# Retention's state products cut into two halves of 64 tokens, on four quadrants of the array

## The chip, the cores and the metric

The kernel runs on one NeuronCore of a Trainium2 chip. Its engines run beside each other and wait for one another by semaphores: TensorE (PE, with its weight loads as PEld), VectorE (DVE), ScalarE (ACT), GpSimd (POOL) and SyncE (SP, which issues the DMAs). The metric is the device time of one execution in microseconds (us), lower is better.

## The reference, cut to what matters

Three layers follow one another: a retention over 768 tokens in 2 batches and 8 heads of 64, then a softplus layer (512 to 2048 to 512), then a SwiGLU layer. The change touches only the retention:

```python
for t in range(S):                                    # S = 768
    state = gamma * state + einsum('bhd,bhe->bhde', k[:, :, t], v[:, :, t])
    y[:, :, t] = scale * einsum('bhd,bhde->bhe', q[:, :, t], state)
```

## The kernel before

The 768 tokens of a batch are cut into 6 chunks (CPB) of 128, so that there are 12 chunks g = 0 to 11 in the program; c is the chunk's number in its batch. A chunk goes through these steps, each of which is a function:

- `turn` (L536) transposes q and k on TensorE; `turned` (ScalarE, L543) and L538 (VectorE) copy them out of PSUM as `at`.
- `scores` (L555) multiplies them into two banks `sc`; its `masked` (VectorE, L559, two instructions of 128x512) writes the masked scores to SBUF, also called `at`.
- `update` (L565 to L583) forms the chunk's addition to the state. It has 8 products, one for each head: the stationary operand is k, 128 tokens by 64, the moving one v, 128 tokens by 64. Two heads share a column of the 128x256 result `u`, one on partitions 0 to 63 and one on 64 to 127. Then `added` writes the new state: a copy where c is 0 (L580), else `u` plus the faded old state (L582). The last chunk of a batch has no update, so that there are 10.
- `fade` (GpSimd, L592) multiplies the new state by the decay, for the next `added`.
- `outputs` (L607) forms y in two banks: first the old state times q, 64x64 weights with 128 moving columns on the four quadrants of the array (`y<-at,state`), where c is over 0; then the masked scores times v (`y<-at,v`, 128x64 weights). The first product of the first kind writes bank 0 of the two, the second bank 1.

In the trace each product of these has two rows on TensorE, so an update has 16.

Chunks 0 to 3 are written out singly (L697 to L751). In the first two the update follows the y products and the scores follow it; in chunk 2 it stands between the scores and the y products; in chunk 3 between the y products and the first product of the next layer (`h`, L645). Chunks 4 to 11 go in pairs through `batch` (L753): transposes of both chunks, scores of both, updates of both, then the outputs of both. In `batch` VectorE's order behind the first update is written out: `added` of the first chunk, one instruction for the weights of a later layer (L433, in two of the four batches), `masked` of the second chunk, and so on. Between the batches stand products `h` of the first layer. From 71.5 us on a planner orders the rest (L960).

PSUM has 8 banks. `bank` hands out the one that was taken longest ago:

```python
oldest = list(range(8))                 # L289
def bank(name, to=oldest):
    i = oldest.pop(0)
    to.append(i)
```

So each further bank that is taken moves all the later ones along, and what a product must wait for is whoever read that bank last.

Of the kernel before, what the change touches and what calls it, by code (L numbers as in the profile page):

```python
# [12 lines left out]
ALU = mybir.AluOpType  # L13
# [240 lines left out]
def retention_softplus_swiglu(ctx: ExitStack, tc: tile.TileContext, q, k, v, w_in, w_out,  # L254
                              w_gate, w_val, w_out2, rms_g, decay, out):
    nc = tc.nc
    B, H, S, D = q.shape
# [8 lines left out]
    NP = H // 2  # L266
# [24 lines left out]
# [3 lines that stand above are left out]
        return ps.tile([P, N], F32, tag=f"ps{i}", name=name)  # L294
# [26 lines left out]
    faded = fd[:, 2 * CPB * H + P:2 * CPB * H + P + NP * D].rearrange("p (j d) -> p j d", j=NP)  # L321
# [243 lines left out]
    def update(g):  # L565
        c = g % CPB
        kk, vv = qkv[g][1], qkv[g][2]
        if c == CPB - 1:
            return lambda: None
        u = bank("u")[:, 0:NP * D].rearrange("p (j t) -> p j t", j=NP)  # L570
        for j in range(NP):
            for e in range(2):
                h = 2 * j + e
                nc.tensor.matmul(u[e * D:(e + 1) * D, j, :], lhsT=kk[:, h, :], rhs=vv[:, NP * e + j, :],  # L574
                                 start=True, stop=True, skip_group_check=True)

        def added():
            new = state[(c + 1) % 2]
            if c == 0:
                nc.vector.tensor_copy(new, u)  # L580
            else:
                nc.vector.tensor_tensor(out=new, in0=u, in1=faded, op=ALU.add)  # L582
        return added  # L583

    def step_u(g):
        update(g)()
        qkv.pop(g)
# [141 lines left out]
    for do in (low32, size, shift, bits):  # L729
        do()  # L730
    masked = scores(3)
    added = update(2)
    added()
    total()
# [10 lines left out]
    nc.sync.dma_start(out=rg, in_=rms_g.rearrange("(k p) -> p k", p=P))  # L745
    parted = outputs([3])
    added = update(3)
    parted()
    added()
# [497 lines left out]
    def lone_gated(nm, f):  # L1247
        h = psum(f"h_{nm}")
        project(h, weight_of(nm, f), XN)
        key = LONE, f  # L1250
        if nm == "w_gate":
            t = pr[key] = r2("t")
            if LONE not in root:
                moved("A", t, h)
                waiting.append(lambda: (less(t, t, root[LONE], ALU.mult), silu(t)))
                return
            else:
                add("V", V_2, lambda e: nc.vector.tensor_tensor(out=t.tile, in0=h.tile, in1=root[LONE].tile, op=ALU.mult),
                    reads=[h, root[LONE]], writes=[t], opens=[t])
            silu(t)  # L1260
        else:
            t = pr[key]
            add("V", V_2, lambda e: nc.vector.tensor_tensor(out=t.tile, in0=h.tile, in1=t.tile, op=ALU.mult),
                reads=[h, t], writes=[t])
            split(key, t)
# [124 lines left out]
    for p in range(NPR):  # L1390
        g, v = Gated("w_gate", p), Gated("w_val", p)
        h = [lambda f=f, nm=nm: lone_gated(nm, f) for nm in ("w_gate", "w_val") for f in (2 * p, 2 * p + 1)]
# [17 lines left out]
    p = NPR - 1  # L1410
# [47 lines left out]
```

## Time and profile before

| | us |
|---|---|
| three runs | 597.4, 595.6, 597.35 |
| their median | 597.35 |
| the profiled execution | 596.97 |
| span of its trace, first to last instruction | 595.2 |
| TensorE busy | 588.4 (99% of the span) |
| VectorE busy | 502.5 (84%) |
| granted TensorE clock, mean | 0.999 |

The page's busy shares are means over the whole span. The retention takes the first 71.5 us; what the change does is read from that stage, and the stage behind it says whether a delay stays.

### The profile page before, as it was taken

The page shows a single profiled execution, that of the slowest core. Times are in us where ns is not written, and L with a number is a line of the kernel's source. Part 1 is how long each engine was busy: PE and PEld are TensorE (multiplying, and loading weights), DVE is VectorE, ACT ScalarE, POOL GpSimd, SP SyncE. Part 2 cuts the span into 40 slices and gives each one's busy share as a digit, 9 for nine tenths or more (in the row PEclk, how much of TensorE's full clock was granted, in tenths as well). Part 3 has the DMA queues.
Part 4 walks back from the last instruction along what each step waited for, and adds up shares of the span by engine and source line. Part 5 has one row for each costly group of instructions (what it writes and reads, how often), then busy time and mean ns, then how long its engine had stood idle before and what let it go on. Part 6 is the DMA issues. An engine that isn't in the chain of part 4 may idle for free.

```text
span 595.2 us, 8619 instructions
## 1 busy us (share of the span) xinstructions
PE 588.4 (99%) x3196; PEld 489.8 (82%) x3196; DVE 502.5 (84%) x881; ACT 358.0 (60%) x634; POOL 123.8 (21%) x99
## 2 busy tenths in 40 slices
PE   9999999999999999999999999999999999999997
PEld 8788888888888888888888888888888888888885
DVE  5787779999998798979999999897897699998455
ACT  3457597689877884869665565654464345544320
POOL 3544231113122112121110012301301122211000
PEclk9999999999999999999999999999999999999999
DMA  9999131114224222231220022312302132200014
GB/s 200 230 231 226 42 111 67 37 35 143 70 78 135 72 70 67 75 107 36 72 70 1 2 70 72 106 36 72 112 30 72 35 107 72 81 26 1 0 54 159
DMA packets 65561, 48.84 MB, mean 82 GB/s; under 512 B 39792, under 2 KB 60528, under 8 KB 65520
## 3 DMA queue, kind: packets, MB, share of 16 engines
q1 hardware_dynamic: 64320, 47.90, 28.2%
q8 instruction: 25, 0.41, 0.3%
q10 hardware_dynamic: 1200, 0.39, 0.3%
q14 instruction: 16, 0.13, 0.1%
HBM read 45.14 MB, written 3.15 MB: 81 GB/s over the span
## 4 chain that ended last, share of the span: by engine, by line
PE 86%; DVE 7%; ACT 4%; DMA 1%; issue 0%; DVEq 0%
PE l L960 31%; PE Q L960 15%; PE R L960 8%; PE h L960 6%; PE h_w_gate L960 6%; PE h_w_val L960 5%; PE W L960 4%; PE y L607 3%; PE h L645 3%; PE sc L555 2%; PE pt L536 2%; DMA st_w_val<-in_moe_w_val_dram 1%; DVE t L984 1%; PE u L574 1%; DVE g L856 1%; DVE x L1034 1%
## 5 line engine op out<-in xcount | busy, mean ns | idle before, releaser
L914 POOL TENSOR_TENSOR c<-w,c 128x512 uint32<-128x512 uint32 x63 | 93.8, 1494 | 382.3 <-DVE w L911 252.4
L960 PE MATMUL l<-g,ws_w_out 128*128 128x512 f32 x576 | 136.2, 389 | 0.0
L960 PEld LDWEIGHTS l<-g,ws_w_out 128*128 128x128 f32 x576 | 108.0, 188 | 22.4
L960 PE MATMUL l<-ws_w_out,g 128*128 128x512 f32 x432 | 108.0, 389 | 0.0
L960 PEld LDWEIGHTS l<-ws_w_out,g 128*128 128x128 f32 x432 | 81.1, 188 | 16.8
L860 ACT ACTIVATE g<-t 128x512 fp32r<-128x512 f32 x78 | 48.3, 628 | 43.5 <-DVE t L856 19.7
L856 DVE TENSOR_TENSOR g<-t,g 128x512 fp32r<-128x512 f32 x78 | 52.9, 689 | 2.6 <-ACT g L860 2.6
L960 PE MATMUL Q<-T,ws_s 128*128 128x512 f32 x216 | 54.3, 389 | 0.0
L860 ACT ACTIVATE p<-Q 128x512 f32<-128x512 f32 x43 | 25.7, 598 | 45.5 <-PE Q L960 45.4
L960 PE MATMUL h<-x,ws_w_in 128*128 128x512 f32 x216 | 51.2, 390 | 0.0
L916 DVE SCALAR_TENSOR_TENSOR a<-a,c 128x512 f32<-128x512 f32 x63 | 44.1, 707 | 5.7 <-POOL c L914 5.6
L960 PEld LDWEIGHTS h<-x,ws_w_in 128*128 128x128 f32 x216 | 40.4, 188 | 8.8 <-DVE t L984 0.3
L960 PEld LDWEIGHTS Q<-T,ws_s 128*128 128x128 f32 x216 | 40.5, 188 | 8.4
L1312 DVE TENSOR_TENSOR o<-l,o 128x512 f32<-128x512 f32 x39 | 26.8, 688 | 16.3 <-PE l L960 16.3
L960 PE MATMUL h_w_val<-x,ws_w_val 128*128 128x512 f32 x144 | 34.7, 390 | 0.0
L960 PE MATMUL h_w_gate<-x,ws_w_gate 128*128 128x512 f32 x144 | 34.6, 390 | 0.0
L960 PEld LDWEIGHTS h_w_gate<-x,ws_w_gate 128*128 128x128 f32 x144 | 27.0, 188 | 5.6
L960 PEld LDWEIGHTS h_w_val<-x,ws_w_val 128*128 128x128 f32 x144 | 27.0, 188 | 5.6
L860 ACT ACTIVATE ws_s<-s 128x512 fp32r<-128x512 f32 x36 | 22.4, 626 | 12.5 <-DVE s L856 11.5
L960 PE MATMUL R<-T,ws_s 128*128 128x512 f32 x108 | 27.2, 389 | 0.0
L856 DVE TENSOR_TENSOR ws_s<-s,ws_s 128x512 fp32r<-128x512 f32 x36 | 25.4, 706 | 1.4 <-ACT ws_s L860 1.4
L982 ACT ACTIVATE t<-t 128x512 f32<-128x512 f32 x42 | 26.3, 628 | 0.4
(172 smaller groups left out, 1062.2 us busy)
## 6 DMA issues: line engine op xcount, KB each, us to landing
st_w_out<-in_moe_w_out_dram SPq DMA_DIRECT2D x28, 512.0 KB, 3.3
st_w_in<-in_moe_w_in_dram SPq DMA_DIRECT2D x16, 512.0 KB, 4.0
st_w_gate<-in_moe_w_gate_dram SPq DMA_DIRECT2D x12, 512.0 KB, 3.6
st_w_val<-in_moe_w_val_dram SPq DMA_DIRECT2D x12, 512.0 KB, 3.9
v<-in_v_dram SPq DMA_DIRECT2D x12, 256.0 KB, 4.9
q<-in_q_dram SPq DMA_DIRECT2D x23, 128.0 KB, 4.6
k<-in_k_dram SPq DMA_DIRECT2D x23, 128.0 KB, 3.9
out_dram<-o SPq DMA_DIRECT2D x11, 256.0 KB, 2.0
```

The costliest lines, as they stand in the source:

```text
L536: nc.tensor.transpose(pt[:, j, :], pair(qkv[g][i], j), ident)
L555: nc.tensor.matmul(sc[e][:, j, :], lhsT=t[r, 1, j, :], rhs=t[r, 0, j, :], start=True, stop=True)
L574: nc.tensor.matmul(u[e * D:(e + 1) * D, j, :], lhsT=kk[:, h, :], rhs=vv[:, NP * e + j, :], start=True, stop=True, skip_group_check=True)
L607: nc.tensor.matmul(ys[e][h * D:(h + 1) * D, i, n * P:(n + 1) * P], lhsT=lhsT, rhs=rhs, start=(e, h) not in begun, stop=last, skip_group_ch ...
L645: nc.tensor.matmul(h, lhsT=w[:, i, kk * P:(kk + 1) * P], rhs=src[j][kk // 2][:, kk % 2, :], start=(n == 0), stop=(n == 3 * KC - 1))
L856: {"V": nc.vector, "G": nc.gpsimd}[eng].tensor_tensor(out=out, in0=in0, in1=in1, op=op)
L860: nc.scalar.activation(out=out, in_=src, func=AF.Copy)
L914: add("G", G_2, lambda e: nc.gpsimd.tensor_tensor(out=c.tile, in0=w.tile, in1=c.tile, op=ALU.add), reads=[w, c], writes=[c])
L916: add("V", V_2, lambda e: nc.vector.scalar_tensor_tensor(out=a.tile, in0=a.tile, scalar=TINY, in1=c.tile.bitcast(F32), op0=ALU.is_ge, op1= ...
L960: nc.tensor.matmul(bank.tile, lhsT=lhsT(), rhs=rhs(), start=starts and k == 0, stop=stops and k == n - 1, skip_group_check=True)
L982: add("A", A_SB, lambda e: nc.scalar.activation(out=t.tile, in_=t.tile, func=AF.Exp, scale=-1.0), reads=[t], writes=[t])
L1312: add("V", V_2, lambda e: nc.vector.tensor_tensor(out=o[2](), in0=bank.tile, in1=o[2](), op=ALU.add), reads=[bank, o[:2]], writes=[o[:2]])
```

## The change

Each of the 10 updates is cut along the 128 tokens into two halves of 64. A product is now 64 tokens by 64, so that there are 16 of them, and they go over the four quadrants of the array in the order (0,0), (1,1), (0,1), (1,0) of (half of the tokens, head of the pair). The two halves of the tokens go to two banks, `us[0]` and `us[1]`, where there was one. `added` does what it did with `us[0]`, and one more instruction adds `us[1]` (L583).

```diff
-        u = bank("u")[:, 0:NP * D].rearrange("p (j t) -> p j t", j=NP)
+        us = [bank("u")[:, 0:NP * D].rearrange("p (j t) -> p j t", j=NP) for _ in range(2)]
         for j in range(NP):
-            for e in range(2):
-                h = 2 * j + e
-                nc.tensor.matmul(u[e * D:(e + 1) * D, j, :], lhsT=kk[:, h, :], rhs=vv[:, NP * e + j, :],
+            for r, e in ((0, 0), (1, 1), (0, 1), (1, 0)):
+                s = slice(r * D, (r + 1) * D)
+                nc.tensor.matmul(us[r][e * D:(e + 1) * D, j, :], lhsT=kk[s, 2 * j + e, :], rhs=vv[s, NP * e + j, :],
                                  start=True, stop=True, skip_group_check=True)
 
         def added():
             new = state[(c + 1) % 2]
             if c == 0:
-                nc.vector.tensor_copy(new, u)
+                nc.vector.tensor_copy(new, us[0])
             else:
-                nc.vector.tensor_tensor(out=new, in0=u, in1=faded, op=ALU.add)
+                nc.vector.tensor_tensor(out=new, in0=us[0], in1=faded, op=ALU.add)
+            nc.vector.tensor_tensor(out=new, in0=us[1], in1=new, op=ALU.add)
         return added
```

VectorE in the batch of chunks 6 and 7, before (the `at` written from `sc_630` and `sc_631` is chunk 6's, from `sc_642` and `sc_643` chunk 7's):

```order
L559 TENSOR_TENSOR at_599<-sc_630,mask_94 128x512
L559 TENSOR_TENSOR at_599<-sc_631,mask_95 128x512
L580 COPY state_66<-u_655 128x256
L433 SCALAR_TENSOR_TENSOR a_593<-a_593,c_592 128x512
L559 TENSOR_TENSOR at_614<-sc_642,mask_94 128x512
L559 TENSOR_TENSOR at_614<-sc_643,mask_95 128x512
```

And there in the changed program (`sc_692` and `sc_693` are now chunk 7's):

```order
L559 TENSOR_TENSOR at_649<-sc_680,mask_94 128x512
L559 TENSOR_TENSOR at_649<-sc_681,mask_95 128x512
L580 COPY state_66<-u_705 128x256
L583 TENSOR_TENSOR state_66<-u_706,state_66 128x256
L433 SCALAR_TENSOR_TENSOR a_643<-a_643,c_642 128x512
L559 TENSOR_TENSOR at_664<-sc_692,mask_94 128x512
L559 TENSOR_TENSOR at_664<-sc_693,mask_95 128x512
```

The new addition stands between the copy and chunk 7's masks; nothing else moved.

TensorE in the same batch, from chunk 7's update on, with the engines that a row waits for, before (`v_559` is chunk 7's v, `v_432` chunk 6's):

```order
L574 MATMUL u<-v_559,k_429 64x64 [waits DMAHW4_49,Pool_49]
L574 MATMUL u<-v_559,k_429 64x64 x7
L607 MATMUL y<-at,state 64x128 [waits DVE_49]
L607 MATMUL y<-at,state 64x128 [waits PE_49]
L607 MATMUL y<-at,state 64x128 x6
L607 MATMUL y<-at,v_432 64x128 x8
L607 MATMUL y<-at,v_559 64x128 [waits DVE_49]
L607 MATMUL y<-at,v_559 64x128 x3
L607 MATMUL y<-at,v_559 64x128 [waits DVE_49]
```

And in the changed program (`v_609` is chunk 7's v, `v_472` chunk 6's):

```order
L574 MATMUL u<-v_609,k_469 64x64 [waits DMAHW4_49,PE_49,Pool_49]
L574 MATMUL u<-v_609,k_469 64x64 [waits DVE_49]
L574 MATMUL u<-v_609,k_469 64x64 x14
L608 MATMUL y<-at,state 64x128 [waits DVE_49]
L608 MATMUL y<-at,state 64x128 [waits DVE_49,PE_49]
L608 MATMUL y<-at,state 64x128 x6
L608 MATMUL y<-at,v_472 64x128 x8
L608 MATMUL y<-at,v_609 64x128 x4
L608 MATMUL y<-at,v_609 64x128 [waits DVE_49]
```

The second `y<-at,state` product now waits for VectorE, and the first `y<-at,v_609` no longer does: a wait has moved up by a step. By the order in which `bank` hands them out, the second y bank is now the one that held the first scores of chunk 7 (before: the first scores of chunk 6).

TensorE in the batch of chunks 8 and 9, behind the updates, before (`v_718` is chunk 9's v):

```order
L607 MATMUL y<-at,state 64x128 [waits PE_49]
L607 MATMUL y<-at,state 64x128 [waits DVE_49]
L607 MATMUL y<-at,state 64x128 x6
L607 MATMUL y<-at,state 64x128 [waits DVE_49]
L607 MATMUL y<-at,state 64x128 x7
L607 MATMUL y<-at,v_716 64x128 x8
L607 MATMUL y<-at,v_718 64x128 [waits DVE_49]
L607 MATMUL y<-at,v_718 64x128 x3
L607 MATMUL y<-at,v_718 64x128 [waits DVE_49]
```

And in the changed program (`v_788` is chunk 9's v):

```order
L608 MATMUL y<-at,state 64x128 [waits DVE_49]
L608 MATMUL y<-at,state 64x128 [waits DVE_49,PE_49]
L608 MATMUL y<-at,state 64x128 x14
L608 MATMUL y<-at,v_786 64x128 x8
L608 MATMUL y<-at,v_788 64x128 x4
L608 MATMUL y<-at,v_788 64x128 [waits DVE_49]
```

Here too the wait of the first product with chunk 9's v is gone, and the second y bank is now the one that held the first scores of chunk 9 (before: of chunk 8). In the batches of chunks 4 and 5 and of chunks 10 and 11 the y banks come from work that is older. From 71.5 us on the order of every engine is the same in both programs.

## Rows read from the trace of the kernel before

**Rows 1.** The page: busy us, share of the span, instructions of each engine.
```profile
PE 588.4 (99%) x3196; PEld 489.8 (82%) x3196; DVE 502.5 (84%) x881; ACT 358.0 (60%) x634; POOL 123.8 (21%) x99
```

**Rows 2.** Chain of waits: start, us, what.
```profile
14.74 0.47 PE u L574 x16
...
19.53 0.61 PE u L574 x16
...
41.85 0.44 DVE state L580
...
42.33 2.56 PE y L607 x48
```

**Rows 3.** Windows: stretch, length, busy of PE, PEld, DVE, ACT, POOL, clock, DMA share, GB/s.
```profile
10.00:60.00 50.00, 48.86 (x689) 42.17 (x687) 39.25 (x70) 27.61 (x52) 23.37 (x24) 1.00 1.05 228
...
71.50:590.00 518.50, 517.79 (x2301) 428.68 (x2300) 449.58 (x789) 320.61 (x566) 93.79 (x63) 1.00 0.20 66
```

**Rows 4.** Timeline, PE, chunk 1: start, us, operation, shape, rows.
```profile
13.05 0.67 PE L607 MATMUL y<-at,state 64*64 64x128 f32 x16
13.65 1.09 PE L607 MATMUL y<-at,v 128*64 128x128 f32 x16
14.58 0.63 PE L574 MATMUL u<-v,k 128*64 128x64 f32 x16
```

**Rows 5.** Windows, PE alone, chunk 1's state products (x: rows in flight).
```profile
13.25:13.31 0.06, 0.06 (x8) 1.00 1.44 226
13.31:13.35 0.03, 0.03 (x12) 1.00 1.47 256
```

**Rows 6.** Timeline, DVE, chunk 0 and the first weight: start, us, operation [idle before <- releaser].
```profile
11.35 0.41 DVE L580 COPY state<-u 128x256 f32<-128x256 f32 x1
12.13 1.29 DVE L559 TENSOR_TENSOR at<-sc,mask 128x512 f32<-128x512 f32 x2 [0.37 <-PE sc L555]
...
18.14 0.42 DVE L409 TENSOR_SCALAR w<-st_w_in 128x512 uint32<-128x512 uint32 x1
18.59 0.69 DVE L413 SCALAR_TENSOR_TENSOR w<-st_w_in,w 128x512 uint32<-128x512 uint32 x1
```

**Rows 7.** Timeline, DVE, ACT and PE, chunks 2 and 3 up to the first h.
```profile
20.26 0.42 DVE L582 TENSOR_TENSOR state<-u,fd 128x256 f32<-128x256 f32 x1 [0.98 <-PE u L574]
20.60 1.28 DVE L559 TENSOR_TENSOR at<-sc,mask 128x512 f32<-128x512 f32 x2
...
21.80 0.68 DVE L433 SCALAR_TENSOR_TENSOR a<-a,c 128x512 f32<-128x512 f32 x1
...
22.51 0.63 ACT L425 ACTIVATE ws_w_in<-a 128x512 fp32r<-128x512 f32 x1 [0.32 <-DVE a L433]
23.05 0.77 ACT L350 ACTIVATE x<-y 128x256 fp32r<-128x256 f32 x2
...
23.78 3.06 PE L645 MATMUL h<-x,ws_w_in 128*128 128x512 f32 x12
...
27.75 0.69 DVE L538 TENSOR_TENSOR at<-pt,tab 128x512 f32<-128x512 f32 x1 [0.87 <-PE pt L536]
```

**Rows 8.** Timeline, DVE and PEld, chunks 4 and 5: the state, chunk 5's state products.
```profile
31.38 0.42 DVE L582 TENSOR_TENSOR state<-u,fd 128x256 f32<-128x256 f32 x1 [0.34 <-PE u L574]
...
31.85 0.42 PEld L607 LDWEIGHTS y<-at,state 64*64 64x64 f32 x16 [0.24 <-DVE state L582]
```

**Rows 9.** Timeline, PEld, chunk 11's state products.
```profile
69.04 0.42 PEld L607 LDWEIGHTS y<-at,state 64*64 64x64 f32 x16 [0.17 <-DVE state L582]
```

**Rows 10.** Timeline, DVE, chunks 6 and 7: behind the copy.
```profile
42.19 0.68 DVE L433 SCALAR_TENSOR_TENSOR a<-a,c 128x512 f32<-128x512 f32 x1
42.79 0.68 DVE L559 TENSOR_TENSOR at<-sc,mask 128x512 f32<-128x512 f32 x1
```

**Rows 11.** Timeline, DVE and PE, chunks 8 and 9.
```profile
55.06 0.42 DVE L582 TENSOR_TENSOR state<-u,fd 128x256 f32<-128x256 f32 x1 [0.23 <-PE u L574]
55.41 0.68 DVE L559 TENSOR_TENSOR at<-sc,mask 128x512 f32<-128x512 f32 x1
...
55.41 1.10 PE L607 MATMUL y<-at,state 64*64 64x128 f32 x32
```

## The prediction, made before the changed kernel ran

> **What bounds the kernel now.** I read the page first: TensorE is busy for 99% of the span [rows 1]. A busy TensorE need not be at its peak, so the next view is the chain of waits. Through the retention it lies on TensorE almost without a break, and leaves it for VectorE only in a few places, as at 41.85 us, where the y products wait for the state [rows 2]. Then the windows, for what lies behind: from 71.5 to 590 us TensorE is busy for 517.79 of 518.50 us, at the full clock [rows 3]: it stands for 0.71 us in all. So whatever the retention ends later, the program ends later by nearly as much; no more than those 0.7 us could be absorbed. DMA is full from 10 to 60 us (share 1.05) [rows 3], which is a rival below.
>
> **The products themselves: nothing.** An update has 16 rows now and takes 0.47 us of the chain where no change of tile shape lies ahead of it [rows 2]: eight pairs, about 58 ns each, two column halves at a time. It will have 32 rows of half the height. Whether four quadrants run at once is shown by the state products: 16 rows of 64x64 with 128 moving columns take 0.60 us to the start of the next group (13.05 to 13.65), the column halves with the same columns 0.93 (13.65 to 14.58) [rows 4]; and within some 35 ns the rows in flight go from 8 to 12, four more [rows 5]. 32 rows in fours are eight groups of 64 columns, so 0.47 us again. This is the best that follows from the rows. The other end is that they run in pairs as now: 16 pairs, 0.94 us. No row shows 64 columns on quadrants; I take 0.47, as the quadrants did halve the time at 128 columns, and keep the other end as a rival.
>
> **Changes of tile shape: +0.28 us.** An update costs 0.61 us between scores and state products, and 0.47 behind y products of its own shape [rows 2], so that a change of shape costs about 0.14 us. Updates 0, 1 and 3 stand behind y products of 128x64 and now get a change ahead of them (+0.14 each); update 2 and those in the batches stand ahead of state products of 64x64 and lose one. In chunks 2 and 3 the two cancel. In the batches the state products wait for VectorE anyway (below), so nothing is gained there. Chunks 0 and 1 leave +0.28; if the step to the scores became cheaper too, 0.
>
> **The new addition.** It has the shape of the one before it, 0.42 us, and needs its result. A dependent pair on VectorE starts 0.45 us apart (18.14 and 18.59, after an instruction of 0.42 us) [rows 6]; so what follows on VectorE, and whoever waits for the state, is 0.45 us later. Bounds: 0.34, the step between independent ones (20.26 to 20.60 [rows 7]), and 0.5.
>
> Chunks 0 and 1: the copy starts at 11.35, the next instruction, which waits for the scores, at 12.13 [rows 6]. That is 0.78 us, and the addition fills 0.45 + 0.34 = 0.79. With the scores 0.14 later it is hidden; chunk 1 repeats the pattern. Cost 0.
>
> Chunks 2 and 3: behind the state at 20.26 VectorE has no gap, so L433 moves from 21.80 to 22.25, ScalarE's L425, which waits for it, from 22.51 to 22.96, and behind that in ScalarE's queue the first half of chunk 3's x from 23.05 to 23.50. It is done at 23.50 + 0.39 = 23.89, and h can start about 0.05 later, 23.94, against 23.78 now [rows 7]: **+0.16**. GpSimd's decay behind this chain makes chunk 3's state later too, by 0.45 and again 0.45, but VectorE stands idle for 0.87 us ahead of 27.75 [rows 7], and that state is not needed before 31 us: 0.
>
> Chunks 4 and 5: chunk 5's state products start at 31.85, released by a state that ends at 31.38 + 0.42 = 31.80 [rows 8]: **+0.45**. Chunk 11's state products, at 69.04, are released in the same way [rows 9]: **+0.45**.
>
> **The moved banks.** This is the largest part, and it comes from the second bank, not from the addition. In the batch of chunks 6 and 7 the second state product now writes the bank of chunk 7's first scores, and has to wait until VectorE has masked them. That instruction starts at 42.79 and takes 0.68 [rows 10]; with the addition ahead of it 43.24, end 43.92. About 0.05 us pass from VectorE's end to TensorE's start (31.80 to 31.85 [rows 8]), so 43.97 where the products now start at 42.33 [rows 2]: **+1.64**. All else on TensorE stands behind it in its queue: y with v, then h. In chunks 8 and 9 the masks of chunk 9 start at 55.41 and take 0.68; with the addition 55.86, end 56.54, TensorE 56.59 against 55.41 [rows 11]: **+1.18**. The addition's 0.45 is within both. The masks' other halves follow 0.6 us later and are needed only behind 1.3 us of other products, as now.
>
> The Trainium skill, TensorEngine Tiling (Array Packing), Restrictions and Gotchas, warns of just this: row tiling increases PSUM pressure, since different row tiles write to different banks. It gives no time for it; the two waits above are what it would be here.
>
> **The sum.** 0.28 + 0.16 + 0.45 + 1.64 + 1.18 + 0.45 = 4.16 us, all on TensorE's path, none of it taken back behind 71.5 us. Against the profiled execution, 596.97 us (span 595.2 and 1.77 around it): **601.1 us**. The median of the three runs is 597.35, within 0.4 of it. The bounds of the small terms (shape changes 0 to 0.5, step of the addition 0.34 to 0.5) give 600.0 to 602.3.
>
> **Rivals.**
>
> *The bank waits cost little.* The wait could be met sooner than I think, if TensorE's waits took VectorE's earlier instructions for enough. For it: the names of the engines, not the instruction waited for, stand in the order. Against: the wait of the first product with chunk 7's (and 9's) v is gone from its place, which is so only where an earlier product already waited for that mask. Then chunks 6 and 7 cost 0.45 (the state alone) and chunks 8 and 9 about 0.1: 0.28 + 0.16 + 0.45 + 0.45 + 0.10 + 0.45 = 1.89, 598.9 us.
>
> *Four quadrants do not run at once with 64 columns.* Each update takes up to 0.47 us more. It counts in eight places (chunks 0 to 3, and the first update of each batch, which VectorE waits for; the second ones of two batches are covered by the bank waits): 3.8 us, 604.9 us. For it: twice as many rows are to be issued in the same time as anywhere in this trace. Against: the 128-column groups came four at a time [rows 4, 5]. The Trainium skill, TensorE: Matmul & The Clock Gate, in the section on 56 ns, has a rule that speaks for it: start to start never falls below some 25 ns however few the columns. By that, as an estimate, 32 rows take 0.80 us, 0.33 more in each of eight places, 603.7 us. The trace does not bear it out: four rows started within some 35 ns [rows 5].
>
> *Not slower: the transfers set the pace of the retention.* The DMA share is 1.05 from 10 to 60 us [rows 3]. If q, k and v came only just in time, TensorE's delays up to there would be spent waiting for them anyway, and the time would stay near 597. It decides where a product waits for a landing. Against it: the chain has no DMA piece in this stage, and each start that I moved is released by VectorE or ScalarE [rows 2, 7 to 9].
>
> **How the numbers follow.** What a measurement here can tell from no change is about 0.3%, 1.8 us. Forecast 601.1: chance 0.74. Bank waits cheap, 598.9: 0.08, half of it under the bound. Quadrants not at once, 602.5 to 604.9: 0.12. Transfers, 597: 0.04. Something unseen that is faster by more than the bound: 0.02. The range that leaves out no more than 2 in 10 reaches down to the second case and into the third: 598.8 to 604.0. Slower 0.90, same 0.07, faster 0.03.
>
> **What the profile of the changed kernel would show.** Updates of 32 rows in about 0.5 us; if they take 0.9, the second rival. TensorE idle for over 1 us ahead of the state products of chunks 7 and 8, released by the masks (L559); if the state (L583) releases them, the first rival. VectorE's new rows at 0.42 us, 0.45 behind the one before. The planned stage starting near 75.7 instead of 71.5 us, and as long as before. If that start is later by 4 us and the end is not, TensorE did not bound what follows, and the reading of the windows was wrong [rows 3].

## The result, and the profile after

The changed kernel takes 601.46 us (median of 4 runs, 601.42 to 601.71) against 596.97 (4 runs): a ratio of 1.008, 95% interval 1.0062 to 1.0098. It is slower, by some 4.5 us; the forecast was 601.1 in a range of 598.8 to 604.0. The profiled execution took 601.71 us, with a span of 600.0 (before: 596.97 and 595.2). One run of e1 (657.65 us) and one of e3 (848.87) were far slower at a low clock; they don't count in the ratios below.

The page of the kernel after; columns as in [rows 1].

```profile
PE 589.2 (98%) x3356; PEld 489.7 (82%) x3356; DVE 505.5 (84%) x891; ACT 357.9 (60%) x634; POOL 124.1 (21%) x99
```

TensorE has 160 rows more and is busy for only 0.8 us more; VectorE has 10 instructions more. The share of TensorE falls from 99 to 98%: it waits. Where is told by the chain of waits of the kernel after (start, us, what), which answers to [rows 2]:

```profile
15.02 0.62 PE u L574 x32
...
19.96 0.69 PE u L574 x32
...
43.89 0.68 DVE a L433
44.57 0.61 DVE at L559
45.19 0.14 issue
45.32 2.56 PE y L608 x46
...
58.09 0.42 DVE state L582
...
58.53 0.02 DVEq L583
...
58.60 0.42 DVE state L583
59.02 0.61 DVE at L559
59.63 0.14 issue
59.77 3.29 PE y L608 x62
...
76.82 0.43 PE h L961
```

An update of 32 rows takes 0.62 behind y products, where 16 rows took 0.47: twice the rows cost a change of shape and no more. In the batches the chain now leaves TensorE twice for L559, VectorE's masks of the scores: the bulk of the output products of chunks 6 and 7 starts at 45.32 instead of 42.33, that of chunks 8 and 9 at 59.77 instead of 55.41, and the planned stage starts at 76.82 instead of 71.61.

The timeline around the two batches (start, us, instruction, rows, idle before and who ended it); [rows 10] and [rows 11] are its counterparts:

```profile
43.02 0.42 DVE L580 COPY state<-u 128x256 f32<-128x256 f32 x1 [0.28 <-PE u L574]
43.55 0.42 DVE L583 TENSOR_TENSOR state<-u,state 128x256 f32<-128x256 f32 x1
43.89 0.68 DVE L433 SCALAR_TENSOR_TENSOR a<-a,c 128x512 f32<-128x512 f32 x1
44.49 1.28 DVE L559 TENSOR_TENSOR at<-sc,mask 128x512 f32<-128x512 f32 x2
...
44.03 0.43 PE L608 MATMUL y<-at,state 64*64 64x128 f32 x2 [0.59 <-DVE state L583]
45.32 0.66 PE L608 MATMUL y<-at,state 64*64 64x128 f32 x14 [0.86 <-DVE at L559]
...
58.31 0.38 PE L608 MATMUL y<-at,state 64*64 64x128 f32 x2
59.77 1.39 PE L608 MATMUL y<-at,state 64*64 64x128 f32 x30 [1.08 <-DVE at L559]
```

L583 is the new addition. It starts 0.53 us behind the copy it depends on, and what follows it 0.34 behind it. In each of the two batches one state product (two rows) goes ahead, into the first bank; the second writes the second bank and waits for the mask. The windows of the retention and of what lies behind it (columns as in [rows 3], TensorE alone):

```profile
10.00:60.00 50.00, 45.59 (x774) 1.00 1.06 226
...
75.80:594.80 519.00, 519.00 (x2322) 1.00 0.20 66
```

The 0.7 us that TensorE stood for in the planned stage of the kernel before are gone: that much of the delay is taken back there.

For a closer reading every run is cut at the same six places of the chain: the start of chunk 2's scores, of the four projections h and of the planned stage. What each stretch takes beyond the same stretch of the kernel before, in us:

| | chunks 2/3 | 4/5 | 6/7 | 8/9 | 10/11 | sum |
|---|---|---|---|---|---|---|
| forecast | 0.16 | 0.45 | 1.64 | 1.18 | 0.45 | 3.88 |
| after | 0.15 | 0.57 | 1.82 | 1.65 | 0.58 | 4.77 |
| e1, banks only | 0.00 | -0.04 | 1.38 | 0.78 | 0.03 | 2.15 |
| e2, addition only | 0.07 | 0.50 | 0.53 | 0.12 | 0.47 | 1.69 |
| e3, without the addition | 0.63 | 0.65 | 1.28 | 2.32 | 0.00 | 4.88 |
| e4, other y bank | 0.30 | 0.51 | 0.55 | 4.64 | 0.53 | 6.53 |
| e5, products only | 0.10 | -0.02 | 0.04 | 4.72 | 0.03 | 4.87 |
| e7, two at a time | 0.57 | 0.77 | 2.07 | 1.58 | 0.79 | 5.78 |
| e8, in step | 0.15 | 0.58 | 3.44 | 1.58 | 0.53 | 6.28 |
| e9, later chunks only | 0.00 | 0.50 | 5.08 | 1.28 | 0.54 | 7.40 |
| e10, changed again | 0.15 | 0.57 | 1.83 | 1.93 | 0.55 | 5.03 |
| e11, in step again | 0.16 | 0.57 | 3.43 | 1.35 | 0.54 | 6.05 |
| e12, later weights | 0.16 | 0.57 | 0.54 | 2.04 | 0.54 | 3.85 |
| e13, before, later weights | -0.01 | -0.04 | 0.07 | 0.01 | -0.01 | 0.02 |

Ahead of these, chunks 0 and 1 took 0.40 more in the kernel after, from the first scores (7.40 before, 7.44 after) to those of chunk 2 (18.36, 18.80). From the planned stage's start to TensorE's last product every program that was late takes 518.7 to 518.8 us, the kernel before 519.7. So a delay gives back 1.0 us there, whether it is e2's 1.7 or e4's 6.5. It comes in two places: 0.2 near 270 us, which e13 without a delay has as well, and 0.8 at the products Q at 313 us, where TensorE of the kernel before waits 0.7 us for VectorE.

### The profile page after: what moved, and what is told of

Its sections match the earlier page's. It is cut to its first block, busy times and chain, and to the rows that moved or that the text cites. A ratio compares the mean times of both kernels' runs of the same rounds, so it can differ in the third digit from the quotient of the medians.

```text
span 600.0 us, 8960 instructions
## 1 busy us (share of the span) xinstructions
PE 589.2 (98%) x3356; PEld 489.7 (82%) x3356; DVE 505.5 (84%) x891; ACT 357.9 (60%) x634; POOL 124.1 (21%) x99
## 4 chain that ended last, share of the span: by engine, by line
PE 97%; DVE 2%; issue 0%; ACT 0%; DVEq 0%
PE l L961 38%; PE Q L961 16%; PE h L961 8%; PE R L961 8%; PE h_w_gate L961 5%; PE h_w_val L961 5%; PE W L961 4%; PE h L646 3%; PE y L608 2%; PE sc L555 2%; PE pt L536 2%; PE u L574 1%; DVE at L559 1%; PE busy L489 0%; PE ms L1184 0%; DVE state L582 0%
```

## Experiments

The theory to test: the loss is two moved banks, a dependent addition that whoever needs the state waits for, and changes of shape. The rivals: the addition alone, or the smaller products themselves. Each trace is of a single execution; the medians are over all runs of a kernel, the profiled one among them.

**e1: the banks alone.** In the kernel before, one more bank is taken at each update and left unused.

```diff
         u = bank("u")[:, 0:NP * D].rearrange("p (j t) -> p j t", j=NP)
+        oldest.append(oldest.pop(0))
```

> The kernel before, with one more PSUM bank taken and left unused at each update; products and VectorE's work as before. Theory (the moved banks, the dependent addition and the changes of shape each cost their own part): nothing moves up to chunk 5; the state products of chunk 7 wait for the masks of chunk 7 and start 1.3 us later, those of chunks 8 and 9 0.8 to 1.1 us later; the planned stage starts at 73.7 to 74.0 us instead of 71.61, and the time rises by 1.7 to 2.4 us, to 598.7 to 599.4. Rival (the addition makes the wait, a bank is free in time): no wait for the masks, the planned stage at 71.6 to 71.8, the time within 0.3 us of before.

Measured: 598.06 us against 596.46, ratio 1.0021 (1.0009 to 1.0033). The timeline of TensorE in e1 shows the kernel after's picture without its products and its addition:

```profile
42.17 0.43 PE L608 MATMUL y<-at,state 64*64 64x128 f32 x2
43.46 0.66 PE L608 MATMUL y<-at,state 64*64 64x128 f32 x14 [0.86 <-DVE at L559]
...
56.50 0.43 PE L608 MATMUL y<-at,state 64*64 64x128 f32 x2
57.32 0.89 PE L608 MATMUL y<-at,state 64*64 64x128 f32 x24 [0.39 <-DVE at L559]
```

The waits for L559 are there: 1.38 and 0.78 us in the table, and nothing elsewhere. The planned stage starts at 73.54, a little under the 73.7 expected, in an execution whose chunk 2 started 0.2 earlier; the time is 0.6 under the expectation, which left out the 1.0 us given back later. The banks are a cause of their own; the rival falls.

**e2: the addition alone.** The kernel before, with the product added a second time.

```diff
                 nc.vector.tensor_tensor(out=new, in0=u, in1=faded, op=ALU.add)
+            nc.vector.tensor_tensor(out=new, in0=u, in1=new, op=ALU.add)
```

> The kernel before, with the same product added to the new state a second time (so each chunk's update counts twice in the state from the second chunk on); banks and matmuls as before. Theory: about 0.5 us each in chunks 4/5, 6/7 and 10/11, 0.2 in chunks 2/3, 0.1 in chunks 8/9: the planned stage starts at 73.2 to 73.7 us and the time rises by 1.2 to 1.9 us, to 598.2 to 598.9. Rival (the addition makes nearly all of the loss): the planned stage at 76 us or later, the time 600.5 to 601.5. Rival (VectorE's work is hidden, the banks make nearly all of it): 71.6 to 71.8 us, 597.

Measured: 597.24 us against 596.46; the ratio, 1.0001 (0.9982 to 1.0020), does not tell it from no change. In the trace the planned stage starts at 72.99. The timeline of VectorE in chunks 6 and 7, where an independent instruction follows the pair:

```profile
42.09 0.42 DVE L580 COPY state<-u 128x256 f32<-128x256 f32 x1 [0.27 <-PE u L574]
42.55 0.42 DVE L583 TENSOR_TENSOR state<-u,state 128x256 f32<-128x256 f32 x1
42.89 0.68 DVE L433 SCALAR_TENSOR_TENSOR a<-a,c 128x512 f32<-128x512 f32 x1
```

Here the pair is 0.46 apart, not 0.53 as in the kernel after. Nine of the ten pairs of the kernel after are 0.52 or 0.53 apart, all ten of e2 0.45 or 0.46; what goes with the difference is told below. The steps are as expected, 0.5 in three places, and their sum, 1.69, lies within the 1.2 to 1.9 expected; the time stays under 598.2, since 1.0 us is given back in the planned stage. By the trace both rivals fall: the addition costs something, and far from 5 us. Two more lines, of the chain of e2 in chunks 6 and 7, are needed below:

```profile
42.98 0.14 issue
43.12 2.57 PE y L608 x48
```

**e3: without the addition.** The changed kernel, its quadrants and its banks, less the line that adds the second half.

```diff
-            nc.vector.tensor_tensor(out=new, in0=us[1], in1=new, op=ALU.add)
```

> The changed kernel without its second addition (the state leaves out tokens 64 to 127 of each chunk): quadrants and banks as changed. Theory: the loss of the moved banks and of the changes of shape is left: the planned stage starts at 74.0 to 74.9 us, the time is 599.0 to 599.8. Rival (the addition makes the loss): the planned stage at 72.0 or earlier, 597.0 to 597.5.

Measured: 600.29 us, ratio 1.0044 (1.0021 to 1.0067), 0.5 us above the expectation; the planned stage starts at 76.35, 1.4 us above it. Chunks 6/7 cost 1.28, as in e1, but chunks 8/9 cost 2.32. Chunks 2/3 and 4/5 cost 0.63 and 0.65, more than with the addition. The chain of e3 shows a stop that no theory had:

```profile
58.64 0.84 PE y L607 x18
59.48 1.13 issue
60.60 2.55 PE y L607 x44
```

"issue" is time in which the engine waited for nothing that the profile shows.

**e4: another bank for y.** The changed kernel, with a second y bank in the two batches that is free earlier.

```diff
-    def bank(name, to=oldest):
-        i = oldest.pop(0)
+    def bank(name, to=oldest, k=0):
+        i = oldest.pop(k)
...
-        ys = [bank("y")[:, 0:2 * w].rearrange("p (i t) -> p i t", i=2) for _ in range(2)]
+        k = 2 if gs[0] in (6, 8) else 0
+        ys = [bank("y", k=k * e)[:, 0:2 * w].rearrange("p (i t) -> p i t", i=2) for e in range(2)]
```

> The changed kernel, but the second output bank of chunks 6/7 and of chunks 8/9 is another: that of the first half's product of chunk 6, or of chunk 8, which is free when that half has been added. Theory: no wait for masks in chunks 6/7, the state products start right behind the second addition (1.3 to 1.4 us earlier); in chunks 8/9 they start 1.0 to 1.1 us earlier: the planned stage starts at 74.0 to 74.7 us instead of 76.82, the time is 598.8 to 599.5. Rival (the wait for the masks only hides another of the same length, VectorE being behind): the state products start at most 0.3 us earlier, the time 601 to 601.5.

Measured: 600.40 us, ratio 1.0064 (1.0036 to 1.0093). In chunks 6/7 it did what was expected: 0.55 instead of 1.82, the addition alone. In chunks 8/9 it lost 4.64. The chain of e4:

```profile
43.69 2.56 PE y L609 x48
...
56.83 1.03 PE y L609 x21
57.86 2.53 issue
60.39 4.03 PE y L609 x43
```

and its windows there (stretch, length, TensorE's busy time and rows, granted clock, DMA share, GB/s):

```profile
57.90:60.30 2.40, 0.00 (x0) 0.97 0.60 121
60.50:64.40 3.90, 3.90 (x44) 0.61 0.03 7
64.50:68.00 3.50, 3.50 (x16) 1.00 0.00 0
```

TensorE stands for 2.5 us where it stood for 1.1 in e3, and behind that its granted clock is 0.50 for a while (0.61 in the mean of the second window): the same products take 4.03 instead of some 2.5 us. Its runs without a profile spread to match: four within 598.6 to 599.0, as the theory had it, the others at 600.4 and above. The bank chosen here is not to blame, since e3 stops there without it. In the trace's records of TensorE (weight loads, products and the sequencer's own instructions counted together) the stop stands at the 1729th, in e3 and in e4; e3 has shorter gaps, some 0.5 us from start to start, at the 705th and the 961st, in chunks 2/3 and 4/5: 193 and two, three and six times 256. TensorE's 6,500 to 6,800 records go with 25 or 26 packets of 16 KB in the DMA queue for instructions, some 260 records to a packet.

**e5: the products only**, e4 and e3 in one, to see the stop without bank waits and without the addition.

```diff
-            nc.vector.tensor_tensor(out=new, in0=us[1], in1=new, op=ALU.add)
...
+        k = 2 if gs[0] in (6, 8) else 0
+        ys = [bank("y", k=k * e)[:, 0:2 * w].rearrange("p (i t) -> p i t", i=2) for e in range(2)]
```

> The changed kernel without its second addition (the state leaves out tokens 64 to 127 of each chunk) and with the second output bank of chunks 6/7 and 8/9 chosen as in e4: what is left of the change are the quadrant products, twice as many rows on TensorE. In e3 and e4 TensorE stood still in the output products of chunks 8/9, for 1.1 and 2.5 us, with nothing that the trace shows it waiting for, both times at about the 1729th of its recorded instructions, a multiple of 256 behind shorter gaps at the 705th and the 961st. Theory (its instructions come in blocks of 256, and with 16 more rows an update that block is wanted before it is there): it stands still at the same instruction again and goes on at 60.2 to 60.7 us; the planned stage starts at 75.4 to 76.4 us, the time is 598.2 to 600.5 and spreads by over 1 us. Rival (the stop belongs to the bank or to the addition): no stop, the planned stage starts at 71.9 to 72.6 us, the time is 596.5 to 597.3.

Measured: 598.70 us, ratio 1.0032 (1.0010 to 1.0053); its runs go from 596.0 to 600.9. The chain of e5:

```profile
56.61 2.54 issue
59.15 4.17 PE y L608 x43
```

The stop stands at the 1729th record again. TensorE goes on 1.1 us earlier than the theory said, as it had come to these chunks 1.2 us earlier than in e4 (45.08 against 46.26 at the third h). The planned stage starts at 76.54. Behind chunk 1 and apart from chunks 8/9 the smaller products cost 0.15 us in all, and its quickest run, 596.03, is no slower than the kernel before beside it (median 596.51).

**e9: only the later chunks changed**, e4 with the updates of chunks 0 to 3 as before, so that TensorE has 128 records fewer ahead of chunk 8.

```diff
+            if g < 4:
+                for e in range(2):
+                    nc.tensor.matmul(us[0][e * D:(e + 1) * D, j, :], lhsT=kk[:, 2 * j + e, :], rhs=vv[:, NP * e + j, :],
+                                     start=True, stop=True, skip_group_check=True)
+                continue
...
```

> e4 with the updates of chunks 0 to 3 left as in the kernel before (128 tokens, one bank, one addition); from chunk 4 on quadrants, two banks and the second addition as in e4, in the same banks. TensorE has 128 recorded instructions fewer ahead of chunk 8, so that a multiple of 256 falls into the projection behind the output products of chunks 8/9 and no more into these. Theory (the instructions' blocks): no stop in the output products of chunks 8/9; the planned stage starts at 73.3 to 73.8 us, the time is 597.6 to 598.5 and spreads by less than 0.8 us. Rival (the stop belongs to those products, whatever came before): a stop of over 1 us there, the planned stage at 75 us or later, the time over 599.

Measured: 600.07 us, ratio 1.0050 (1.0028 to 1.0072). The expectation of the time was wrong: the stop left chunks 8/9, as the theory said, and came in chunks 6/7 instead. The chain of e9:

```profile
43.48 0.92 PE y L615 x17
44.41 2.51 issue
46.92 3.68 PE y L615 x31
...
62.24 3.16 PE y L615 x64
```

It stands at the 1217th record, which is 193 and four times 256. I had reckoned with one multiple only; with 128 records fewer another one fell into dense products. The stop kept to a multiple of 256 when the program ahead of it got shorter, which is what the blocks predict and the rival does not. The low clock behind it reaches into the next stretch: 1.28 in chunks 8/9.

**e12: less for the DMA to move.** e4, with one load of weights (512 KB) moved behind the last loads of q, k and v.

```diff
-    loads((8, 2), (9, 2), (10, 0), (10, 1), None)
+    loads((8, 2), (9, 2), (10, 0), (10, 1))
...
-    loads((11, 0), (11, 1), None)
+    loads((11, 0), (11, 1))
...
-    loads((10, 2), (11, 2))
+    loads((10, 2), (11, 2), None, None)
```

> e4 with one load of weights (512 KB) moved from ahead of the last loads of q, k and v to behind them, so that the DMA queues have less to move between 51 and 58 us. In e4 the block of instructions that TensorE waited for was fetched at 57.4 us, 5 us behind the crossing into the block before it, with the DMA engines at 0.95 to 1.15 of their time, and TensorE went on 3.0 us behind the fetch. Theory (the fetch waits behind the loads): the fetch comes 1 to 2 us earlier, the stop in the output products of chunks 8/9 is 0 to 1.2 us instead of 2.5, the clock stays at 1.00 there, the median is 598.6 to 599.6 us. Rival (the fetch does not depend on the loads): a stop of over 2 us, median 600 or more, as e4.

Measured: 598.98 us, ratio 1.0027 (1.0006 to 1.0048). The chain of e12:

```profile
56.82 1.03 PE y L609 x21
57.85 1.41 issue
59.25 2.55 PE y L609 x43
```

The packet of instructions starts at 56.57 us instead of 57.55, the stop is 1.41 instead of 2.53, the clock stays at 1.00, and the same 43 rows take 2.55 instead of 4.03. The stop was a little longer than the 1.2 expected. In all five executions with a stop of over 1 us TensorE went on 2.7 to 3.0 us behind the packet's start (57.63 and 60.60 in e3, 57.55 and 60.39 in e4, 56.36 and 59.15 in e5, 44.12 and 46.92 in e9, 56.57 and 59.25 in e12).

**e13: the control.** The same move of the loads in the kernel before (its diff is that of e12).

> The kernel before with the load of weights moved as in e12, a control for e12. Theory (in the kernel before every block of instructions is there in time, so the loads' order does not matter): no stop in chunks 6 to 9, the planned stage at 71.3 to 71.8 us, the median within 0.4 us of the kernel before, 596.0 to 596.8. Rival (the move of the load saves time by itself, and e12 owes its gain to that): 1 us or more below the kernel before, 595.4 or less.

Measured: 596.46 us against 597.56 beside it, ratio 0.9987 (0.9966 to 1.0008), the planned stage at 71.60, every stretch within 0.07. So the move does nothing by itself that these runs can tell, and e12's gain over e4 goes with the shorter stop. That rests on one trace of each; the ratios, 1.0027 and 1.0064, have intervals that overlap. The runs bear it out: all ten of e12 have a mean granted clock of 0.999 or 1.000, e4's five above 600 us 0.994 to 0.998.

**e8 and e11: no row ahead.** The changed kernel with the quadrants of a state product in another order, so that the first row is the one that waits for the moved bank.

```diff
-                    for e, h in ((0, 0), (1, 1), (0, 1), (1, 0)):
+                    for e, h in ((1, 1), (0, 0), (0, 1), (1, 0)):
```

> The changed kernel with the four quadrants of a state product taken in the order (1,1), (0,0), (0,1), (1,0), so that the row that waits for the moved bank is the first one and no two rows go ahead of it. Theory (two rows ahead put the quadrants out of step, 0.3 us): the output products of chunks 8/9 take 0.1 to 0.3 us less from the release on, those of chunks 6/7 0.1 less. Rival (the instructions' block sets when these rows end): the products of chunks 8/9 end when they did, and the time is 601.4 to 601.7.

Measured: 603.16 us in a single run. I was after 0.3 us in chunks 8/9, where the products took 3.23 us from the release on instead of 3.29, and found 1.6 lost in chunks 6/7. The windows of e8 there:

```profile
43.40:45.10 1.70, 0.00 (x0) 1.00 0.57 115
45.20:49.30 4.10, 4.10 (x49) 0.58 0.97 213
49.40:52.00 2.60, 2.60 (x12) 1.00 1.26 223
```

The wait for the bank is as long as in the kernel after, 1.9 us in all, but with no two rows inside it. TensorE's granted clock falls to 0.50 behind it (0.58 in the mean of the second window), and the y products take 4.18 us instead of 2.56. e11 is the same kernel with more runs, beside e10, the changed kernel again.

> The kernel of e8 once more, with more runs. In e8 TensorE's granted clock fell to 0.50 in the output products of chunks 6/7, behind an unbroken wait of 1.8 us for the moved bank; in the changed kernel two products stand within that wait and the clock stays at 1.00. Theory (the unbroken wait costs the clock, run after run): median 602.6 to 603.4 us, 1.2 to 1.8 us above e10, the profiled run again at 0.50 there. Rival (the clock fell by chance in that one run): median 601.2 to 601.8.

> The changed kernel once more, beside e11 and e12, for the spread of its runs. Theory (its waits for the two moved banks come where TensorE would else stand still for want of instructions, and are short enough to leave its clock alone): median 601.3 to 601.8 us, all undisturbed runs within 1 us. Rival (it meets the same stops as e4): runs spread over 3 us or more, as in e4.

Measured: e11 602.75 us (602.61 to 603.16), e10 602.02 (601.32 to 603.62). In e11 the clock fell again in the same place, and chunks 6/7 cost 3.43, as in e8 (3.44), against 1.82 and 1.83. Each of e11's four runs has a mean granted clock of 0.995 to 0.997; of e10's four, three have 0.999 or 1.000, and the slowest 0.997. So that is no chance. The medians are 0.7 apart instead of 1.2 to 1.8: e10's median is above the 601.3 to 601.8 expected, its runs spread over 2.3 us, more than the 1 expected and less than its rival's 3, and chunks 8/9 gave some back to e11 (1.35 against 1.93). e10's chain has a stop of 0.18 us in chunks 8/9, at the 1729th record.

**e7: two quadrants at a time.** The changed kernel, with an update's rows in the order of all (0,0) and (1,1), then all (0,1) and (1,0).

```diff
-        for j in range(NP):
-            for r, e in ((0, 0), (1, 1), (0, 1), (1, 0)):
+        for pairs in (((0, 0), (1, 1)), ((0, 1), (1, 0))):
+            for j in range(NP):
+                for r, e in pairs:
...
```

> The changed kernel with each update's products in another order: for all eight pairs of heads the quadrants (0,0) and (1,1), then for all eight the quadrants (0,1) and (1,0). Theory (a group of four quadrants goes at once, and the next row of a quadrant waits for the one before it): an update takes 16 steps of 58 ns, 0.93 us instead of 0.47, and as VectorE's additions start that much later, the planned stage starts 2 to 4 us later, the time is 603 to 605. Rival (rows of different quadrants do not need to stand in groups of four): an update takes the same 0.47 us, the time is 601.3 to 601.8.

Measured: 602.95 us in a single run. The first update in the timeline of e7, and in that of the kernel after:

```profile
10.12 0.98 PE L575 MATMUL u<-v,k 64*64 64x64 f32 x32
```

```profile
10.59 0.69 PE L574 MATMUL u<-v,k 64*64 64x64 f32 x32
```

It is 0.91 us to the next group (which starts at 11.03) instead of 0.62 (11.21): the pairs do not run as four, though a little quicker than the 58 ns a pair that was expected, for the change of shape is in the 0.91 as well. The planned stage starts 1.1 us later than in the kernel after, not 2 to 4: the second updates of the batches run beside VectorE's work.

## Why the prediction was right, point by point

**The products themselves, nothing: right.** An update of 32 rows behind y products takes 0.62 us, of which 0.15 are the change of shape; e5 shows 0.15 us in all behind chunk 1 and outside chunks 8/9, and e7 that it hangs on rows of four different quadrants standing side by side. The reading that quadrants halve the time was loose: 0.60 against 0.93 us [rows 4] is two thirds. What the step did not see is that twice the rows are twice the instructions (below).

**Changes of shape, +0.28: right.** Updates 0 and 1 cost 0.63 and 0.62 instead of 0.47, 0.31 together; with 0.07 that the first y products started later and 0.02 of small steps, chunks 0 and 1 took 0.40 more.

**Chunks 2 and 3, +0.16: right** (0.15), along the path that was named, from L433 over L425 and the first half of x to h.

**Chunks 4/5 and 10/11, +0.45 each: 0.57 and 0.58.** The step of the dependent addition was taken from a pair of instructions on SBUF data, 0.45 us [rows 6]; nine of the ten new pairs are 0.52 or 0.53 apart, beyond the 0.5 that was given as a bound. The new addition needs both the copy's result and TensorE's second half. In those nine the trace has a wait for a semaphore, run by VectorE's sequencer, between the two instructions (`DVEq L583` in the chain above). The tenth pair (60.73 and 61.18) has none and is 0.45 apart, though it reads two banks too, and e2's ten pairs have none; e2 has 0.50 and 0.47 here.

**The moved banks, +1.64 and +1.18: mechanism right, 1.82 and 1.65.** e1 moved nothing but the banks and the two waits came, released by L559 as foretold. Each term was too small by the 0.08 of the addition's step and by 0.09 of the same kind on TensorE: 0.05 us from VectorE's end to TensorE's start was read where a row waits for VectorE alone [rows 8]; the row that waits for the moved bank waits for VectorE and for TensorE, the trace has a separate wait for a semaphore ahead of it, and it takes 0.14 (45.19 to 45.32, 59.63 to 59.77). It isn't the bank: e2 has the same 0.14, with such a wait, behind the state in chunks 6 and 7 (42.98 to 43.12). That makes 1.81 and 1.35. The remaining 0.30 in chunks 8/9 I put down, before e8 ran, to the two rows that went ahead and left the quadrants out of step. The traces speak against it. e7 has the same two rows ahead and takes no longer than e11, which has none; both lines are of the chains, as is that of the kernel after above (3.29):

```profile
60.94 3.00 PE y L609 x62
```

```profile
60.93 3.00 PE y L608 x64
```

From the release to the first product of scores and v it takes 1.03 us in e1, e7 and e11, and 1.32 in the kernel after, 1.27 in e8 and 1.60 in e10, where the rows are in rhythm up to the 1729th record and out of it behind. So the 0.30 goes with the block of instructions (0.17 us from the 1729th record's start to the next one's; 0.44 in e10, whose stop is the longer), and not with the order of the rows: the sum left out a wait that it couldn't see.

**The bank and the addition do not add up as two separate edits would.** In chunks 8/9 e2 alone costs 0.12, since chunk 8's own products fill the time, and e1 alone 0.78. Together, without a stop, they cost 1.35 (e11): once the bank stops those products, nothing hides the addition.

**None of it taken back behind 71.5 us: wrong by 1.0.** The windows gave 0.7 us that could be absorbed, and the sum took none of it [rows 3]. Every delayed program got 1.0 back, 0.8 of it at the one wait of those 0.7 us. Against that the kernel after has 4.5 us from its last product to the end of the span, before 3.9; among the experiments it is 3.5 (e2, e9) to 4.6 (e10), and what sets it is open. So the sum of 4.16 met the measured 4.5 (4.7 in the profiled executions) with errors against each other: up to the planned stage the loss was 5.21, 1.05 more than the sum; 1.0 of it was given back in that stage; and 0.6 came on top behind the last product. That the total came within 0.4 us is in part luck. The bounds of 600.0 to 602.3 don't follow from the two terms named for them, which give 600.3 to 601.6 (shape changes 0.28 down or 0.22 up, the addition 0.11 down or 0.05 up in five places).

**The rivals.** *Bank waits cheap* fell with e1. *Four quadrants not at once* fell with the 0.62 us of an update. *The transfers set the pace* was wrong as put, since no product of the retention is seen waiting for a landing of q, k or v in the kernel after. But the full DMA had a say that was not foreseen, through the instructions: in e4, without the bank waits, it costs 2.5 us and the clock. In the kernel after the packet starts at 57.83 us, so by the 2.7 to 3.0 us of the other runs the block is there at 60.5 to 60.8; TensorE, which the masks had held up to 59.77, is at its 1729th record at 60.33 and goes on at 60.50, so that most of the wait for the block lies inside the wait for the masks. So of the 1.65 us in chunks 8/9 some would be lost without the moved bank as well: taking the moved bank away (e4) brought the median down by only some 1 to 1.6 us (600.40 against 601.46, and 602.02 in e10), where 2.0 to 2.7 were expected. e12, with less to move in that stretch, is at 598.98. No version with the quadrants and both additions came down to the median of the kernel before.

## What to carry to other kernels

A buffer that an edit takes from a rotation moves every later one: write out for each later use who last used its bank, for that, and not the edit's own work, was here the larger loss (2.15 us alone in e1, the addition 1.69 in e2). More and smaller rows on TensorE can be free in engine time and still cost, because their instructions come by DMA too: where the transfers are at their full share, count the rows between two packets. In e4 the 256 records ahead of the stop took 5.2 us (52.43 to 57.59), in the kernel before the same numbers took 12.0 (56.62 to 68.62), and it didn't stop. An instruction that comes to wait for two semaphores instead of one has a separate wait ahead of it, here 0.07 to 0.09 us. And a wait is not only as long as it is: if nothing stands inside it, the clock may be the price of what follows.

## What was not expected of the hardware

- **Instructions come in blocks.** TensorE stood still at its 1217th or 1729th record (193 and a multiple of 256), for 1.1 to 2.5 us, in dense stretches of small products, with the DMA engines at 0.99 to 1.08 of their time in the 5 to 6 us ahead of the packet; it went on 2.7 to 3.0 us behind the start of a packet of 16 KB in the instruction queue. Moving 512 KB of loads out of the way brought the packet 1.0 us earlier and shortened the stop by 1.1 (e4, e12). What holds the packet back in the queue, and what fills the 2.7 us or more behind it, isn't shown.
- **The clock.** Where TensorE stood without a product for 1.9 us (e8, e11) or 2.5 (e4, e5, e9) the granted clock fell to 0.50, 1.2 GHz, inside the stop or within 0.4 us behind it, for 3.4 us (6.8 in e9), and then was 1.00 again. It stayed at 1.00 in the kernel after, whose wait of the same length holds one product (two rows, 0.43 us), and behind the 1.41 us of e12. In e8 the price was 1.6 us.
- **Two waits.** Where one of the instructions named above waits for two semaphores, the trace has a separate wait ahead of it. A dependent pair on VectorE is 0.45 or 0.46 us apart without one (e2), 0.52 or 0.53 with one (after). From VectorE's end to TensorE's start: 0.05 us without one, 0.14 with one.
- **Quadrants.** In an update of the kernel after, groups of four rows of 64x64 products with 64 columns follow each other every 58 ns, the four of a group starting 6 to 7 ns apart. In e7's order an update takes 0.91 us instead of 0.62.
